# Two transformer layers on one core: weight loads on a second queue, and two buffers moved

## The chip, the cores and the metric

The kernel runs on one core of a Trainium2 chip. A core has five engines, each with its own in-order stream of instructions: TensorE (PE in the profile, matrix products), VectorE (DVE), ScalarE (ACT), GpSimd (POOL) and SyncE (SP), which here issues the transfers between memory and the core. The metric is the device time of one execution in microseconds (us); less is better.

## The reference

Two layers, each an attention block and a feed-forward block, on 2048 rows of 640 numbers:

```python
def _A_ref(x, wqkv, wo):
    H = 32; Dh = D // H; W = 256
    ...
    scores = jnp.einsum("bhqd,bhkd->bhqk", q, k) * (Dh ** -0.5)
    mask = (idx[:, None] - idx[None, :] >= 0) & (idx[:, None] - idx[None, :] < W)
    p = _softmax(jnp.where(mask[None, None], scores, -1e9), axis=-1)
    o = jnp.einsum("bhqk,bhkd->bhqd", p, v)
    return o.transpose(0, 2, 1, 3).reshape(B, S, D) @ wo

def _B_ref(x, w1, b1, w2, b2):
    h = jnp.einsum("bsd,df->bsf", x, w1) + b1
    r = jnp.where(h > 0, h, 0)
    return jnp.einsum("bsf,fd->bsd", r * r, w2) + b2

x = x + _A_ref(_layernorm(x), A_wqkv, A_wo)
x = x + _B_ref(_layernorm(x), B_w1, B_b1, B_w2, B_b2)
```

The last two lines are done twice with the same weights. There are 32 heads of 20 numbers, the window is 256 keys, and the feed-forward width is 1536.

## The kernel before

**Tiling.** The rows are worked on in 16 units of 256 (eight a layer). A unit goes through these stages: layernorm and transposition of its rows (`ln_load`, `ln_t`), query and key products (`stage_qk`), value products (`stage_v`), attention, output product (`stage_o`), second layernorm (`stage_y`) and feed-forward (`stage_f`). Every operand is kept as a pair of 16-bit numbers, high and low part, and every product is made as three (`mm3`, line 256), so each product's result is evicted twice: ScalarE writes the high part, VectorE the low part.

**Attention.** Heads go by fours ("quads", eight a unit). For a quad `max_quad` makes the scores, and VectorE takes the row maxima (line 555). After two quads `max_out` turns the maxima and sends them as two more rows of the queries (line 580). Then `exp_quad` makes the scores anew, less their maxima, ScalarE takes the exponential (line 625), GpSimd masks it (lines 640, 644), and `pv_quad` multiplies by the values (line 674). Scores of both kinds share one pair of memory banks, `bb`. Units 0 and 8 have no unit before them and half as many scores.

**Queries and keys** must change their layout, and do so by way of memory. `leave` (lines 435 to 468) writes the evicted tile `qd` out with two transfers (lines 445, 447) and reads it back with two others (line 451) into `qt` and `kt`. `qd` is a buffer of which there is one. In unit 0 the queries use it, while the keys use part of `hraw`; in units 1 and 2 queries and keys use it one after the other. For later units the keys have a place of their own.

**Output.** `load_o` reads a unit's attention output and its row sums (lines 720, 721), divides (753, 756) and splits into `od` (760, 763), which `stage_o` multiplies by the output weights. For unit 0 `od` lies in `hraw`, columns 1280 to 2560. So its load waits for the third and fourth piece of w2, which were staged there.

**Weights** come as 32-bit numbers into staging places and are converted into pairs (`convert`: ScalarE, then VectorE, or ScalarE again and GpSimd). The attention weights come first. The output weights (five pieces of 320 KB, line 224) and w1 (six of 640 KB, line 232) are staged in the room of w2, and w2 (twelve of 320 KB, line 245) in `hraw`: four places for the first four pieces, then two. `hraw` has the same memory as `hh`, the result of the first feed-forward product, so unit 0's `hh` waits for the last conversion. All of these loads are issued by SP, in between the transfers above.

**Order.** The order of the instructions on each engine is set by a planner in the kernel's own text, which runs when the program is built. `post` puts a job (engine, assumed duration, what it waits for, priority; a lower number goes first) on a list, and `pump` issues what is ready by its clocks. `dma` posts a transfer on SP, whose rate is an assumed number (`rate`); `idle` holds one back until SP's assumed transfers are nearly through. Waits for a buffer to come free are not in this plan: the engine meets them when it runs. TensorE's work is written by generators: `rest` is the chain of projections of units 0 to 2, and `flow` runs unit 0's quads and takes work from `rest` where a quad isn't ready. From unit 1 on `together` deals one unit's quads out evenly over the dense work of its neighbours, which for unit 1 is: what is left of `rest`, then `stage_o(0)`, `stage_y(0)` and `stage_f(0)`. From unit 4 on the rows are transposed by DMA (`ln_cross`, line 355), which `stage_f` starts between its two products; units 0 to 3 are transposed on TensorE (line 300).

The order of quads in unit 0, with m for `max_quad`, r for `max_out`, s for `exp_quad`, v for `pv_quad`, is:

```python
todo = [("m", n) for n in range(GQ)] + [("r", 0)] + [("m", n) for n in range(GQ, LEAD)]
for n in range(NQ):
    todo += [("s", n)] + ([("r", n + LEAD - GQ)] if n % GQ == 1 else []) + [("m", n + LEAD), ("v", n)]
flow(todo, rest)
load_o(0, False, (w2j[2], w2j[3]))
```

with GQ = 2, LEAD = 3 and NQ = 8: quads 8, 9 and 10, the first three of unit 1, have their maxima between unit 0's last quads.

Of the kernel before, what the change touches and what calls it, by code (L numbers as in the profile page):

```python
# [14 lines left out]
ALU = mybir.AluOpType  # L15
# [29 lines left out]
def kernel(ctx: ExitStack, tc: tile.TileContext, x, wqkv, wo, w1, b1, w2, b2, out):  # L45
# [45 lines left out]
    now, clk, pend, moved = [0.0], {"A": 0.0, "D": 2e3, "G": 0.0, "S": 0.0}, [], [0.0]  # L91
    LOOK, LAT, LAND, CROSS, WLAND = 250.0, 50.0, 1800.0, 3600.0, 4500.0
    rate = [335.0]
    TAIL = {"A": 115.0, "D": 85.0, "G": 40.0, "S": 0.0}

    class Job:
        def __init__(self, eng, cost, fn, deps, nb, prio, size=0, idle=False, land=LAND):
            self.eng, self.cost, self.fn, self.deps, self.nb, self.prio = eng, cost, fn, deps, nb, prio
            self.size, self.idle, self.land = size, idle, land
            self.end, self.gates = None, []  # L100
# [4 lines left out]
        def start(self):  # L105
            t = max([clk[self.eng], self.nb] + [d.end + LAT for d in self.deps])
            return max(t, moved[0] - 2200.0) if self.idle else t

        def put(self):
            t = self.start() + self.cost  # L110
            self.fn()
            clk[self.eng] = t
            self.end = t + TAIL[self.eng]
            if self.eng == "S":
                moved[0] = max(moved[0], t) + self.size / rate[0]
                self.end = moved[0] + self.land
            for g in self.gates:
                g.end = self.end
# [73 lines left out]
    def convert(st, hi, low, n, load, *deps, prio=2, dve=True):  # L192

        a = post("A", 20 + 0.9 * n, lambda: nc.scalar.activation(hi, st, AF.Copy, scale=WS), load, *deps, prio=prio)
        if dve:
            return post("D", 30 + 1.04 * n, lambda: nc.vector.scalar_tensor_tensor(low, st, WS, hi, op0=ALU.mult,
                                                                                   op1=ALU.subtract), a, prio=prio)
        b = post("A", 20 + 0.9 * n, lambda: nc.scalar.activation(st, st, AF.Copy, scale=WS), a, prio=prio)
        return post("G", 30 + 2.0 * n, lambda: nc.gpsimd.tensor_tensor(low, st, hi, op=ALU.subtract), b, prio=prio)
# [20 lines left out]
    def load_wo():  # L220
        v = wo.rearrange("(h c d) n -> c d h n", c=KC, d=4)
        for c in range(KC):
            st = w2raw[:, FC * D - (KC - c) * D:][:, :D]
            load = dma(lambda st=st, c=c: nc.sync.dma_start(st, v[c]), P * D * 4, gate0, prio=2, idle=True, land=WLAND)
            woj[c] = convert(st, wo_s[:, 0, c], wo_s[:, 1, c], D, load, dve=False)
        rowset[1] = [post("D", 460, lambda k=k: set_row(1, k), prio=2) for k in range(4)]

    def load_w1():
        first = list(wqj.values())
        for f0 in (0, 6, 2, 8, 4, 10):  # L230
            st = w2raw[:, f0 * D:(f0 + 2) * D].rearrange("p (c n) -> p c n", c=KC)
            load = dma(lambda st=st, f0=f0: nc.sync.dma_start(
                st, w1[:, f0 * P:(f0 + 2) * P].rearrange("(c p) n -> p c n", p=P)), P * KC * 2 * P * 4, gate,
                *(woj.values() if (f0 + 2) * D > (FC - KC) * D else ()), prio=2, idle=True, land=WLAND)
            for f in (f0, f0 + 1):
                c = slice(f * P, (f + 1) * P)
                w1j[f] = convert(st[:, :, (f - f0) * P:(f - f0 + 1) * P], w1_s[:, 0, :, c], w1_s[:, 1, :, c], KC * P,
                                 load, *first, dve=f % 3 == 2)

    def load_w2():  # L240
        for c in range(FC):
            first = [w1j[f] for f in (c // 4 * 2, c // 4 * 2 + 1, 6 + c // 4 * 2, 7 + c // 4 * 2)]
            slot = c if c < 4 else c % 2
            st = hraw[:, D * slot:D * (slot + 1)]
            load = dma(lambda st=st, c=c: nc.sync.dma_start(st, w2[c * P:(c + 1) * P, :]), P * D * 4,
                       *([w2j[c - 4 if c < 6 else c - 2]] if c > 3 else [gate]), prio=2, idle=True,
                       land=WLAND)
            w2j[c] = convert(st, w2_s[:, 0, c], w2_s[:, 1, c], D, load, *first, dve=c % 3 == 2)
# [136 lines left out]
    def stage_qk(u, which=(0, 1)):  # L385
# [7 lines left out]
        for j, c0 in order:  # L393
            if j not in qds:
                if j == 0:
                    qts[u] = sb.tile([P, NP, T], F16, name="qt", tag="qt", bufs=2)
                if j and u == 0:
                    qd = hraw[:, :KC * T].bitcast(F16).rearrange("p (c a n) -> p c a n", a=2, n=T)
                elif j and u > 2:
                    qd = beside(u)[:, 1].rearrange("p (c a n) -> p c a n", a=2, n=T)  # L400
                else:
                    qd = sb.tile([P, KC, 2, T], F16, name="qd", tag="qd", bufs=1)
                qds[j] = qd
# [299 lines left out]
    def load_o(u, late=False, free_=()):  # L703
# [45 lines left out]
        for i in range(4):  # L749
# [15 lines left out]
            j = post("D", 575, ratio, loaded, prio=2)  # L765
            j = post("D", 409, times, j, prio=2)
            j = post("A", 360, high, j, prio=0 if i < 2 else 2)
            js.append(post("D", 402, low, j, prio=2))
# [6 lines left out]
    def stage_o(u):  # L775
        od, x1b, js, xj = ols.pop(u)
        for i in range(2):
# [15 lines left out]
            x1s[u, i], ys[u, i] = x1, (y, layernorm(x1, y, *adds, prio=1))  # L793
# [177 lines left out]
    def flow(todo, dense):  # L971
# [3 lines left out]
        while todo:  # L975
# [4 lines left out]
                     "v": quad[1][0] if quad else []}[kind]  # L980
# [24 lines left out]
    rate[0] = 215.0  # L1005
    ln_load(1)
# [18 lines left out]
    left_over = 3 * (QKC + VC + LNC) - used[0]  # L1025
    rate[0] = 320.0
    for u in range(1, NU):
        last = u == NU - 1
        quads, ahead = range(NQ * u, NQ * (u + 1)), range(NQ * u + LEAD, NQ * (u + 1) + LEAD)
# [50 lines left out]
```

## Time and profile before

| | |
|---|---|
| median of three runs | 1644.63 us (1643.55 to 1646.98) |
| the profiled execution | 1641.93 us |
| its span, first to last instruction | 1640.2 us |
| mean granted clock of TensorE | 0.987 |
| busy: TensorE, VectorE, ScalarE, GpSimd | 96%, 63%, 46%, 39% |

The profile is that of one execution. Times within it count from the span's start. A line such as `L414` is that of the kernel's text; `qd<-acc` means that the tile qd was written from the tile acc; `x20` counts instructions; what stands in brackets behind an instruction is how long its engine was idle before it, and what ended that. SPq is SP's queue, where the time of a transfer is that of its issue, not of the bytes. In a table of stretches each engine has its busy time and its count, and the last three numbers are TensorE's granted clock (1.00 is full), the share of the transfer engines' time, and GB/s.

### The profile page before, as it was taken

Reading aid. Unit: us, or ns where it says so; the run is one execution under the profiler, and the core shown is the slowest. Engines: PE = TensorE matmul, PEld = TensorE weight load, DVE = VectorE, ACT = ScalarE, POOL = GpSimd, SP = SyncE. Lnnn points to the kernel's source line nnn. Section 1 sums busy time; section 2 is a strip of 40 time slices with the busy share of each in tenths; the row PEclk is TensorE's granted clock in tenths of the full one; section 3 lists DMA queues with packets and bytes.
Section 4 is the critical chain, followed back from the end, with each engine's and each line's share of the span. In section 5 each row is a group of like instructions: output and inputs, shape, how many; then the busy total and the mean of one; then the engine's idle time right before and its main releaser. Section 6 shows DMA issues by size and latency. Waiting matters only on the chain.

```text
span 1640.2 us, 52819 instructions
## 1 busy us (share of the span) xinstructions
PE 1575.6 (96%) x21670; PEld 1172.6 (71%) x21670; DVE 1030.1 (63%) x3231; ACT 748.4 (46%) x1616; POOL 636.6 (39%) x1309
## 2 busy tenths in 40 slices
PE   7697899999999999999999999999999999999989
PEld 5564677777777777777777777777777777776667
DVE  7567657675665766566565756657665666757341
ACT  4465534535444454544434354444545444453512
POOL 1343533535344353434414343443534344354412
PEclk9898999999999999999999999999999999999999
DMA  8465214343342434345253434425343452431020
GB/s 255 123 183 157 62 63 109 65 118 86 102 102 65 124 75 112 80 108 114 51 137 74 124 85 103 102 69 119 73 112 81 106 117 51 110 71 54 27 65 17
DMA packets 231517, 157.95 MB, mean 96 GB/s; under 512 B 79468, under 2 KB 215020, under 8 KB 231276
## 3 DMA queue, kind: packets, MB, share of 16 engines
q1 hardware_dynamic: 231276, 154.59, 38.4%
q8 instruction: 170, 2.79, 0.7%
q14 instruction: 71, 0.58, 0.1%
HBM read 84.68 MB, written 52.95 MB: 84 GB/s over the span
## 4 chain that ended last, share of the span: by engine, by line
PE 83%; DVE 6%; ACT 4%; DMA 4%; POOL 2%; issue 1%; SPq 1%; DVEq 0%; ACTq 0%; POOLq 0%
PE acc L256 63%; PE pv L674 10%; PE bb L542 5%; PE bb L613 5%; DVE bb L555 3%; ACT pt L625 2%; DMA qk<-qd 1%; DMA xt<-in_B_b_dram 1%; PE tr L567 1%; POOL x L805 1%; DVE mx L555 1%; POOL pt L644 0%; ACT r L843 0%; DMA w_s<-in_B_w_dram 0%; DMA ov<-o 0%
## 5 line engine op out<-in xcount | busy, mean ns | idle before, releaser
L555 DVE CUSTOM_DVE_ANT_0 bb<-bb,maskb 128x384 f32<-128x384 f32 (+2 forms) x1024 | 510.5, 567 | 114.9 <-PE bb L542 106.4
L625 ACT ACTIVATE pt<-bb 128x512 f32<-128x512 f32 (+1 forms) x736 | 376.5, 601 | 233.9 <-PE bb L613 220.5
L640 POOL TENSOR_SCALAR_AFFINE_SELECT pt<-pt 128x256 f32<-128x256 f32 x448 | 194.8, 439 | 529.7 <-ACT pt L625 507.9
L256 PE MATMUL acc<-y,w_s 128*128 128x256 f16 x2880 | 330.8, 273 | 4.8 <-DVE y L304 1.5
L256 PE MATMUL acc<-w_s,hh 128*128 128x320 f16 x2304 | 326.2, 299 | 0.0
L256 PEld LDWEIGHTS <-w_s 128*128 128x128 f16 x2880 | 277.9, 98 | 57.3 <-issue 23.5
L256 PE MATMUL acc<-yT,wq_s 128*128 128x256 f16 x2400 | 281.0, 275 | 14.0 <-DVE qd L414 11.9
L256 PEld LDWEIGHTS <-hh 128*128 128x128 f16 x2304 | 221.7, 98 | 96.8 <-issue 12.5
L256 PEld LDWEIGHTS <-wq_s 128*128 128x128 f16 x2400 | 232.9, 99 | 57.5 <-issue 26.5
L644 POOL TENSOR_SCALAR_AFFINE_SELECT pt<-pt 128x256 f32<-128x256 f32 x512 | 217.3, 446 | 65.7 <-ACT pt L625 64.6
L853 DVE TENSOR_TENSOR hh<-r,hh 128x256 f16<-128x256 f32 x192 | 91.9, 500 | 205.9 <-ACT hh L850 199.3
L674 PE MATMUL pv<-pt,vt 128*32 128x128 f32 (+1 forms) x3840 | 189.6, 332 | 2.0 <-POOL pt L644 1.4
L847 POOL TENSOR_TENSOR r<-r 128x256 f32<-128x256 f32 x192 | 113.5, 612 | 181.2 <-ACT r L843 179.9
L686 ACT COPY ot<-pv 128x256 f32<-128x256 f32 x128 | 47.6, 372 | 277.4 <-PE pv L674 277.4
L555 DVE DVE_READ_ACCUMULATOR2_ANT mx<- 128x1 f32 x1024 | 145.4, 142 | 0.1
L256 PE MATMUL acc<-wq_s,yT 128*128 128x320 f16 x960 | 142.1, 301 | 0.1
L674 PEld LDWEIGHTS pv<-pt,vt 128*32 128x32 f32 x3840 | 104.4, 110 | 45.6 <-POOL pt L644 4.9
L256 PE MATMUL acc<-wo_s,od 128*128 128x320 f16 x900 | 130.5, 299 | 3.9 <-DVE x L785 1.7
L843 ACT ACTIVATE r<-acc,b1s 128x256 f32<-128x256 f32 x192 | 80.6, 471 | 98.0 <-PE acc L256 97.2
L256 PEld LDWEIGHTS <-yT 128*128 128x128 f16 x960 | 93.1, 99 | 40.4 <-issue 6.5
L256 PEld LDWEIGHTS <-od 128*128 128x128 f16 x900 | 85.5, 98 | 44.7 <-issue 8.3
L613 PE MATMUL bb<-qt,kt 62*64 62x128 f16 (+3 forms) x3840 | 100.3, 235 | 9.1 <-DVE mx L555 8.4
(84 smaller groups left out, 1169.5 us busy)
## 6 DMA issues: line engine op xcount, KB each, us to landing
qt<-qk SPq DMA_DIRECT2D x30, 480.0 KB
kt<-qk SPq DMA_DIRECT2D x30, 480.0 KB
qk<-qd SPq DMA_DIRECT2D x17, 640.0 KB
o<-ot SPq DMA_DIRECT2D x256, 42.0 KB
od<-o SPq DMA_DIRECT2D x13, 640.0 KB
qk<-yl SPq DMA_DIRECT2D x13, 640.0 KB
qk<-qd SPq DMA_DIRECT2D x17, 320.0 KB
xt<-in_A_x_dram SPq DMA_DIRECT2D x16, 320.0 KB
```

What stands on the lines that cost most here:

```text
L256: nc.tensor.matmul(acc, lhs(a, c), rhs(b, c), start=(k == 0), stop=(k == 3 * nk - 1))
L542: nc.tensor.matmul(to, qt[r, p, i * P + 64 * h:i * P + 64 * h + 64], kt[r, p, a:b], start=True, stop=True, tile_position=(64 * e, 64 * h))
L555: nc.vector.tensor_tensor_reduce(out=v, in0=v, in1=mask, scale=1.0, scalar=-3.0e38, op0=ALU.add, op1=ALU.max, accum_out=accum)))
L613: nc.tensor.matmul(bb[e][64 * h:64 * h + 64, k, o:o + w], kt[r, p, ko + 64 * h:ko + 64 * h + 64], qt[r, p, q:q + w], start=True, stop=True ...
L625: nc.scalar.activation(box["pt"][:, :o], bb[e][:, k, :o], AF.Exp, scale=SCALE / (QS * QS))
L640: nc.gpsimd.affine_select(out=m, in_=m, pattern=[[0, 2], [-1, P]], compare_op=ALU.is_gt, fill=0.0, base=0, channel_multiplier=1)
L644: nc.gpsimd.affine_select(out=m, in_=m, pattern=[[0, 2], [1, P]], compare_op=ALU.is_ge, fill=0.0, base=0, channel_multiplier=-1)
L674: nc.tensor.matmul(pv[32 * jj:32 * (jj + 1), q0 * P:(q0 + qn) * P], vf[:, c:c + 32], pj[:, j, :], start=(k == 0), stop=(k == len(steps) - ...
L686: nc.scalar.copy(ot[:, qd % 2], pv)
L843: nc.scalar.activation(box["r"], acc[:, f, :], AF.Relu, bias=b1s[:, f0 + f:f0 + f + 1], scale=1.0 / (YS * WS))
L847: nc.gpsimd.tensor_tensor(box["r"], box["r"], box["r"], op=ALU.mult)
L853: nc.vector.tensor_sub(hh[:, 1, f, :], box["r"], hh[:, 0, f, :])
```

## The change

1. Unit 0's queries too are evicted into `hraw`, behind the keys' part.
2. Output weights, w1 and w2 are issued by ScalarE, through the new `wdma`. The planner keeps a second clock of moved bytes for that queue, with a rate of 100 bytes a ns, a landing time of 6000 ns instead of 4500 and 400 ns of slack ahead of the conversions. SP's transfers are taken to land 2000 ns later until unit 1 is done. The first output weight no longer goes at the earlier gate (unit 0's first keys), but at that of its last. w2 is staged in four places throughout.
3. Unit 0's `od` is a tile in `qd`'s buffer, and its load no longer waits for two conversions. The division and both layernorms around it have a better priority, and so has the layernorm of the rows of units 1 and 2.
4. The first three maxima of unit 1 and their `max_out` stand behind unit 0's last quad and behind `load_o(0)`, not between unit 0's quads.
5. Unit 2's second half of the value products leaves `rest` and goes into `stage_y(0)`, a quarter ahead of each of the two rows' transposes. Unit 3's rows are no longer transposed on TensorE; `stage_f(0)` starts their `ln_cross`.

```diff
-    rate = [335.0]
+    rate = {"S": 335.0, "A": 100.0}
+    late_ = [0.0]
...
-            return max(t, moved[0] - 2200.0) if self.idle else t
+            return max(t, moved[self.eng] - 2200.0) if self.idle else t
...
-            if self.eng == "S":
-                moved[0] = max(moved[0], t) + self.size / rate[0]
-                self.end = moved[0] + self.land
+            if self.size:
+                moved[self.eng] = max(moved[self.eng], t) + self.size / rate[self.eng]
+                self.end = moved[self.eng] + late_[0] if self.eng == "S" else t + self.size / 200.0
+                self.end += self.land
...
+    def wdma(fn, size, *deps):
+
+        return post("A", 450.0, fn, *deps, prio=2, size=size, idle=True, land=WLAND)
...
-            load = dma(lambda st=st, c=c: nc.sync.dma_start(st, v[c]), P * D * 4, gate0, prio=2, idle=True, land=WLAND)
+            load = wdma(lambda st=st, c=c: nc.scalar.dma_start(st, v[c]), P * D * 4, gate)
...
-            load = dma(lambda st=st, f0=f0: nc.sync.dma_start(
+            load = wdma(lambda st=st, f0=f0: nc.scalar.dma_start(
...
-            slot = c if c < 4 else c % 2
+            slot = c % 4
...
-            load = dma(lambda st=st, c=c: nc.sync.dma_start(st, w2[c * P:(c + 1) * P, :]), P * D * 4,
-                       *([w2j[c - 4 if c < 6 else c - 2]] if c > 3 else [gate]), prio=2, idle=True,
-                       land=WLAND)
+            load = wdma(lambda st=st, c=c: nc.scalar.dma_start(st, w2[c * P:(c + 1) * P, :]), P * D * 4,
+                        *([w2j[c - 4]] if c > 3 else [gate]))
...
-                if j and u == 0:
-                    qd = hraw[:, :KC * T].bitcast(F16).rearrange("p (c a n) -> p c a n", a=2, n=T)
+                if u == 0:
+                    qd = hraw[:, (1 - j) * KC * T:][:, :KC * T].bitcast(F16).rearrange("p (c a n) -> p c a n", a=2, n=T)
...
-            od = hraw[:, 2 * D:4 * D].bitcast(F16).rearrange("p (c a n) -> p c a n", a=2, n=T)
+            od = sb.tile([P, KC, 2, T], F16, name="od", tag="qd", bufs=1)
...
+            pr = 2 if u else 0.5
+            j = post("D", 575, ratio, loaded, prio=pr)
+            j = post("D", 409, times, j, prio=pr)
+            j = post("A", 360, high, j, prio=0 if i < 2 else pr)
+            js.append(post("D", 402, low, j, prio=pr))
...
-    def stage_y(u):
+    def stage_y(u, between=()):
...
+            if between:
+                yield from stage_v(*between[i])
...
     def ahead_of(u):
         yield from stage_qk(u)
-        yield from stage_v(u)
-        yield from ln_t(u + 1)
+        yield from stage_v(u, range(4 if u < 2 else 2))
         if u < 2:
-            ln_load(u + 2)
+            yield from ln_t(u + 1)
+        if u < 1:
+            ln_load(u + 2, prio=1.5)
...
-        todo += [("s", n)] + ([("r", n + LEAD - GQ)] if n % GQ == 1 else []) + [("m", n + LEAD), ("v", n)]
+        todo += [("s", n)] + [("r", n + LEAD - GQ)] * (n % GQ == 1 and n + LEAD - GQ < NQ)
+        todo += [("m", n + LEAD)] * (n + LEAD < NQ) + [("v", n)]
+    todo += [("o", 0)] + [("m", NQ + n) for n in range(GQ)] + [("r", NQ)] + [("m", NQ + n) for n in range(GQ, LEAD)]
     flow(todo, rest)
-    load_o(0, False, (w2j[2], w2j[3]))
...
-            parts += [rest, stage_o(0), stage_y(0)]
+            parts += [rest, stage_o(0), stage_y(0, ((2, (2,)), (2, (3,))))]
             cost += LNC + left_over
+            ahead_ln = 3
```

In `flow` the new kind "o" calls `load_o(0)`.

More of the change, by code (lines that the diff above doesn't have):

```diff
@@ L86, with __init__ @@
         set_row(0, k)
-    now, clk, pend, moved = [0.0], {"A": 0.0, "D": 2e3, "G": 0.0, "S": 0.0}, [], [0.0]
-    LOOK, LAT, LAND, CROSS, WLAND = 250.0, 50.0, 1800.0, 3600.0, 4500.0
-    rate = [335.0]
+    now, clk, pend, moved = [0.0], {"A": 0.0, "D": 2e3, "G": 0.0, "S": 0.0}, [], {"S": 0.0, "A": 0.0}
+    LOOK, LAT, LAND, CROSS, WLAND, SLACK = 250.0, 50.0, 1800.0, 3600.0, 6000.0, 400.0
+    rate = {"S": 335.0, "A": 100.0}
+    late_ = [0.0]
     TAIL = {"A": 115.0, "D": 85.0, "G": 40.0, "S": 0.0}
     class Job:
-        def __init__(self, eng, cost, fn, deps, nb, prio, size=0, idle=False, land=LAND):
+        def __init__(self, eng, cost, fn, deps, nb, prio, size=0, idle=False, land=LAND, slack=0.0):
             self.eng, self.cost, self.fn, self.deps, self.nb, self.prio = eng, cost, fn, deps, nb, prio
-            self.size, self.idle, self.land = size, idle, land
+            self.size, self.idle, self.land, self.slack = size, idle, land, slack
             self.end, self.gates = None, []
@@ L105, in start @@
         def start(self):
-            t = max([clk[self.eng], self.nb] + [d.end + LAT for d in self.deps])
-            return max(t, moved[0] - 2200.0) if self.idle else t
+            t = max([clk[self.eng], self.nb] + [d.end + LAT + self.slack for d in self.deps])
+            return max(t, moved[self.eng] - 2200.0) if self.idle else t
         def put(self):
@@ L192, in convert @@
     def convert(st, hi, low, n, load, *deps, prio=2, dve=True):
-        a = post("A", 20 + 0.9 * n, lambda: nc.scalar.activation(hi, st, AF.Copy, scale=WS), load, *deps, prio=prio)
+        slack = SLACK if prio > 1 else 0.0
+        a = post("A", 20 + 0.9 * n, lambda: nc.scalar.activation(hi, st, AF.Copy, scale=WS), load, *deps, prio=prio,
+                 slack=slack)
         if dve:
             return post("D", 30 + 1.04 * n, lambda: nc.vector.scalar_tensor_tensor(low, st, WS, hi, op0=ALU.mult,
-                                                                                   op1=ALU.subtract), a, prio=prio)
+                                                                                   op1=ALU.subtract), a, prio=prio,
+                        slack=slack)
         b = post("A", 20 + 0.9 * n, lambda: nc.scalar.activation(st, st, AF.Copy, scale=WS), a, prio=prio)
-        return post("G", 30 + 2.0 * n, lambda: nc.gpsimd.tensor_tensor(low, st, hi, op=ALU.subtract), b, prio=prio)
+        return post("G", 100 + 2.2 * n, lambda: nc.gpsimd.tensor_tensor(low, st, hi, op=ALU.subtract), b, prio=prio,
+                    slack=slack)
     wqj, woj, w1j, w2j = {}, {}, {}, {}
@@ L231, in load_w1 @@
             st = w2raw[:, f0 * D:(f0 + 2) * D].rearrange("p (c n) -> p c n", c=KC)
-            load = dma(lambda st=st, f0=f0: nc.sync.dma_start(
+            load = wdma(lambda st=st, f0=f0: nc.scalar.dma_start(
                 st, w1[:, f0 * P:(f0 + 2) * P].rearrange("(c p) n -> p c n", p=P)), P * KC * 2 * P * 4, gate,
-                *(woj.values() if (f0 + 2) * D > (FC - KC) * D else ()), prio=2, idle=True, land=WLAND)
+                *(woj.values() if (f0 + 2) * D > (FC - KC) * D else ()))
             for f in (f0, f0 + 1):
@@ L763, in low @@
                 nc.vector.tensor_sub(od[:, :, 1, q], val[:, :, q], od[:, :, 0, q])
[L765 to L768, printed above, removed]
+            pr = 2 if u else 0.5
[3 more added lines that the diff above has]
+            js.append(post("D", 402, low, j, prio=pr))
         ols[u] = od, x1, js, xj
@@ L792, in stage_o @@
             y = sb.tile([P, D], F32, name="xt", tag="xt", bufs=2)
-            x1s[u, i], ys[u, i] = x1, (y, layernorm(x1, y, *adds, prio=1))
+            x1s[u, i], ys[u, i] = x1, (y, layernorm(x1, y, *adds, prio=1 if u else 0.5))
     def add_b2(u):
@@ L979, in flow @@
                      "s": [*bbjobs, *([rowjobs.get((u, G))] if n % GQ == 0 else [])],
-                     "v": quad[1][0] if quad else []}[kind]
+                     "v": quad[1][0] if quad else [], "o": []}[kind]
             if not all(j is not None and j.end is not None and j.end <= now[0] + LOOK for j in wants):
@@ L990, in flow @@
                 max_quad(n)
+            elif kind == "o":
+                load_o(0)
             elif kind == "r":
@@ L1004 @@
     run(ln_t(0))
-    rate[0] = 215.0
-    ln_load(1)
+    rate["S"] = 215.0
+    late_[0] = 2000.0
+    ln_load(1, prio=1.5)
     load_wo()
@@ L1021 @@
     for n in range(NQ):
-        todo += [("s", n)] + ([("r", n + LEAD - GQ)] if n % GQ == 1 else []) + [("m", n + LEAD), ("v", n)]
+        todo += [("s", n)] + [("r", n + LEAD - GQ)] * (n % GQ == 1 and n + LEAD - GQ < NQ)
+        todo += [("m", n + LEAD)] * (n + LEAD < NQ) + [("v", n)]
+    todo += [("o", 0)] + [("m", NQ + n) for n in range(GQ)] + [("r", NQ)] + [("m", NQ + n) for n in range(GQ, LEAD)]
     flow(todo, rest)
-    load_o(0, False, (w2j[2], w2j[3]))
-    left_over = 3 * (QKC + VC + LNC) - used[0]
-    rate[0] = 320.0
+    left_over = 3 * (QKC + VC) + 2 * LNC - used[0]
+    rate["S"] = 320.0
     for u in range(1, NU):
         last = u == NU - 1
+        if u > 1:
+            late_[0] = 0.0
         quads, ahead = range(NQ * u, NQ * (u + 1)), range(NQ * u + LEAD, NQ * (u + 1) + LEAD)
```

## The prediction

> **What bounds the kernel now.** I read the page's engine shares and slices first, then the busy time by stages, then what TensorE waited for, then the chain and the queues around each wait.
>
> ```profile
> span 1640.2 us, 52819 instructions
> ...
> PE   7697899999999999999999999999999999999989
> ```
>
> TensorE is full from the sixth slice on; the open time lies in the first 200 us. By stages (busy time of the engines, then TensorE's granted clock, DMA share, GB/s):
>
> ```profile
> 36.00:58.00 22.00, 20.22 (x261) 15.06 (x260) 18.07 (x83) 8.91 (x19) 5.47 (x8) 1.00 0.52 131
> 58.00:70.00 12.00, 0.38 (x3) 0.26 (x3) 1.09 (x3) 2.30 (x6) 0.52 (x2) 0.56 0.39 140
> 70.00:101.00 31.00, 29.39 (x363) 20.15 (x362) 16.11 (x77) 20.21 (x45) 15.14 (x24) 0.95 0.73 172
> 101.00:127.00 26.00, 20.95 (x313) 15.63 (x314) 21.10 (x66) 15.84 (x30) 12.07 (x16) 0.93 0.51 164
> 127.00:145.00 18.00, 16.13 (x206) 10.36 (x195) 9.89 (x27) 13.04 (x27) 9.67 (x17) 0.90 0.55 162
> 145.00:176.00 31.00, 21.34 (x237) 12.74 (x237) 23.16 (x61) 12.21 (x24) 9.11 (x15) 0.73 0.64 154
> 176.00:198.00 22.00, 20.37 (x302) 16.61 (x302) 11.26 (x35) 15.77 (x36) 15.71 (x28) 1.00 0.09 25
> 260.00:1640.00 1380.00, 1359.49 (x18929) 1016.72 (x18927) 861.14 (x2685) 619.39 (x1353) 543.73 (x1142) 1.00 0.37 88
> ```
>
> Span less the first figure is TensorE's idle time: 11.6, 1.6, 5.0, 1.9, 9.7 and 1.6 us in the six stages from 58 to 198, 31.4 in all. The lowered clock costs at most busy time times what is missing of 1.00: 1.5 + 1.5 + 1.6 + 5.8 = 10.4 us between 70 and 176. So about 42 us lie there to be won; the last stage, 1380 us at 98.5% and full clock, is not touched by the diff. What TensorE waited for up to 260 us (total, times, longest):
>
> ```profile
> PE acc L256 <- DVE qd L414: 11.9, 1, 11.9
> ...
> PE bb L613 <- DVE mx L555: 4.9, 4, 3.0
> PE acc L256 <- ACT stg L760: 4.1, 1, 4.1
> PE tr L300 <- DVE xt L286: 3.1, 1, 3.1
> PE acc L256 <- DVE stg L763: 2.9, 2, 2.1
> ```
>
> **Term 1, the hole at 58 (weights leave SP's queue).** The timelines of SP and ScalarE, and the chain of waits:
>
> ```profile
> 49.38 1.79 SPq L224 DMA_DIRECT2D w_s<-in_A_wo_dram  x3
> 51.22 0.94 SPq L232 DMA_DIRECT2D w_s<-in_B_w_dram  x1
> 52.37 5.42 SPq L445 DMA_DIRECT2D qk<-qd  x1
> 57.83 3.27 SPq L447 DMA_DIRECT2D qk<-qd  x1
> ```
>
> ```profile
> 68.24 0.60 ACT L411 ACTIVATE qd<-acc 128x512 f16<-128x512 f32 x1 [9.70 <-DMA qk<-qd]
> ```
>
> ```profile
> 108.22 6.17 DMA qk<-qd
> ```
>
> Unit 1's queries and keys share the one buffer qd: the first key eviction waits until the query write has left it, ScalarE and VectorE stand behind it in order, and TensorE with both accumulators full. The write was issued behind 1.6 MB of weights and was out only at 68.1; unit 2's write, alone, took 6.2 us. The first edit (unit 0's queries in hraw) does not touch this pair: unit 1 still has one buffer. It only frees qd of unit 0's write, for which no wait shows. What helps is that the weights are elsewhere: issued at 52.4, the write is out near 59; with 0.60 for ScalarE and 0.7 for VectorE TensorE resumes near 60.4 instead of 69.6, having run dry at 57.7. I add 1 us for weights moving beside it: hole 3.7, **gain 8.0**. Ends: 0 (the same bytes finish as late) and 11.6.
>
> **Term 2, 101 to 145 (maxima of unit 1 behind load_o).**
>
> ```profile
> 126.20 0.27 PE L613 MATMUL bb<-qt,kt 62*64 62x256 f16 x1 [3.02 <-DVE mx L555]
> ```
>
> ```profile
> 121.53 0.86 PE L542 MATMUL bb<-kt,qt 60*64 60x128 f16 x36
> ```
>
> ```profile
> 101.00:145.00 44.00, 17.13 (x64) 0.92 0.53 163
> ```
>
> ```profile
> 29.83 6.82 PE L256 MATMUL acc<-wq_s,yT 128*128 128x320 f16 x49
> ```
>
> The second row is one quad's score products, the third VectorE's work at L555 alone: 64 instructions, four quads, 4.3 us a quad. Before, three of these quads lay between unit 0's quads with projection work beside them. Now they stand in a row: 12.9 us of VectorE against 3 x 0.86 = 2.6 us of score products and the half of unit 2's values left in the stream, 30 products of 0.139 us = 4.2. That exposes 6.2 us where 3.3 showed. The transposes of unit 3 leave, with their waits of about 1.1. Together a **loss of 1.8**. Ends: a loss of 7 (no filler stands there), a gain of 6.9 (all hidden). The wait of 1.6 for unit 2's query write stays.
>
> **Term 3, 145 to 176 (od's own place, values ahead of the transposes).**
>
> ```profile
> 124.70 1.58 SPq L691 DMA_DIRECT2D o<-ot  x4
> ...
> 135.53 2.20 SPq L245 DMA_DIRECT2D stg<-in_B_w_dram  x2
> 137.83 0.59 SPq L720 DMA_DIRECT2D rs<-o  x1
> ```
>
> Unit 0's last output left at 126.3, but its load came 11.5 us later, behind w2's loads and for two conversions whose staging od took. Both go. I keep 2 us for landing: 9.5 us earlier. TensorE also arrives earlier at the output product: 4.2 for the values moved away, 2.8 for the transposes and their waits; and later by the maxima now between, 2.6 + 2.9. Net 8.0 us, against 7.0 of waits for od; I leave 1 open. New in its way: od now lies in qd and waits for unit 2's key write; that was issued at 129.4, before load_o, so the load's trip covers it; uncovered it costs the 6.2 above. y2 follows od there, but only after y's layernorm. The values in front of each transpose give 15 products, 2.0 us, against the 3.1 us wait for y: 1.1 left. Idle 9.7 to 2.6, **gain 7.1**; ends 0 and 9.7.
>
> **Term 4, the smaller parts.** Unit 3's ten transposes leave TensorE:
>
> ```profile
> 141.37 0.49 PE L300 MATMUL tr<-ident,xt 128*128 128x128 f32 x3
> 142.42 0.44 PE L300 MATMUL tr<-ident,xt 128*128 128x128 f32 x2 [0.56 <-ACT vt L480]
> 143.39 0.83 PE L300 MATMUL tr<-ident,xt 128*128 128x128 f32 x5 [0.53 <-DVE yT L304]
> ```
>
> **1.7 us gained.** In exchange come two loads of x and four DMA transposes in stage_f(0), hidden behind its second product as for every later unit. w2 comes by four slots throughout: of the 1.6 us at 176 to 198 I count **0.5** (ends 1.6, and a loss of 3 if it comes late). The first output weight, held to the later gate, starts some 1 us later, far ahead of its use: nothing.
>
> The weights' issues go to ScalarE (ns: least, median, most):
>
> ```profile
> L224 SPq DMA_DIRECT2D w_s<-in_A_wo_dram x5: 537/579/707, 35.4 to 50.6; - x5
> L232 SPq DMA_DIRECT2D w_s<-in_B_w_dram x6: 394/399/942, 51.2 to 105.4; - x6
> L245 SPq DMA_DIRECT2D stg<-in_B_w_dram x12: 327/357/1843, 108.8 to 179.7; - x12
> ```
>
> 5 x 0.58 + 6 x 0.40 + 12 x 0.36 = 9.6 us. ScalarE is busy 72.5 of the 140 us from 36 to 176, and behind each issue, and each wait for a staging slot, stand exponentials and evictions. Most fall into its idle half: **cost 1**; ends 0 and 9.6.
>
> **Term 5, the clock.**
>
> ```profile
> 114.00:118.00 4.00, 2.37 (x30) 1.73 (x28) 2.88 (x6) 2.44 (x4) 1.82 (x2) 0.94 0.03 10
> 118.00:122.00 4.00, 3.94 (x47) 2.66 (x48) 2.69 (x7) 3.06 (x8) 2.62 (x5) 0.63 0.01 1
> ```
>
> In the hole from 58 to 70 the clock was 0.56, and 1.6 us of idle time (114 to 118) were enough for 0.63 in the 4 us behind. I let the loss go with idle time: from 58 to 176 there were 29.8 us, left are 3.7 + 1.6 + 8.7 + 2.6 = 16.6; 10.4 x 13.2 / 29.8 = **4.6 gained**; ends 0 and 10.4. The Trainium skill (TensorE: Matmul & The Clock Gate, "What's actually happening") has the clock fall only after a whole idle window of about 3.4 us; by that of what is left only term 1's hole would cost, and the gain would be some 4 us more. The row of 118 to 122, behind 1.6 us, speaks against it.
>
> **Sum.** 8.0 - 1.8 + 7.1 + 1.7 + 0.5 - 1 + 4.6 = 19.1. The profiled execution took 1641.93 us (1.7 around its span); the median of the three runs is 1644.63. Less 19.1 that is 1622.8 by the profiled execution and by the median **1625.5 us**, which I give.
>
> **Rivals.** *A, the transfers share the engines.* The write need not stand behind the weights to be slowed by them: 2.62 MB (1.64 of weights, 0.98 of queries) moved from 49.4 to 68.1, 0.140 MB a us. If the write of 0.98 MB gets half, it takes 14 us, is out at 66.4, and term 1 gives 1.7 and the clock 2.2 less: gain 10.6, 1634. For it: 0.39 of the DMA time was used and yet 140 GB/s moved. Against: 6.17 us in the other row. The Trainium skill (DMA: Bandwidth & Descriptors, "Issuing engines are not separate DMA queues") says that DMAs issued from several engines run on the same 16 and that this saves only the time of issue; by that term 1 would be this rival's. No run shows two queues yet.
>
> *B, slower: ScalarE stands in its own issues.* L445 above held SP 5.42 us with 1.6 MB queued ahead. ScalarE has 67.5 us free from 36 to 176; 23 issues of 2.9 us use it up, and from there the kernel is slower. At 3.5 us each it is 13 us: 1658. Against: the loads are spaced at 100 bytes a ns, and the median issue is 0.4.
>
> *C, everything is covered.* Only 3 us of term 1 and the 1.6 of unit 2 remain: 42 + 1.7 - 4.6 - 1.6 for their clock - 1 = 36: 1608. For it: TensorE has other work at each wait. Against: VectorE's 4.3 us a quad.
>
> *D, the wait moves.* Term 2 loses 7 and term 3 gains only 2: 8 - 7 + 2 + 1.7 + 0.5 - 1 + 1 = 5: 1639.5.
>
> *E, A and D together*: nothing left.
>
> **Chances.** Forecast 0.50, A 0.13, C 0.13, D 0.09, E 0.06, B 0.09. The measurement tells 0.2% (3.3 us) from no change: faster 0.85, same 0.06, slower 0.09. The range from 1607 to 1643 takes in A, C and D and leaves out B and the ends of C and E.
>
> **What would show it.** Term 1: L445 short on SP, the wait of L411 for qk<-qd from 9.7 to 2-4 us (A: 8). Term 2: waits of L613 or L567 for mx over 3 us ahead of the first 32-product L613. Term 3: L720 within 6 us of the last o<-ot, and no wait for L760 or L763 over 2 us. ScalarE's queue: issues of 0.3 to 1 us (B: over 2.9). Term 5: 0.90 or more in all stages behind 70. A hole at a new place, or ScalarE late with exponentials, would prove the forecast wrong.

## The result and the profile after

| | median, us | lowest to highest |
|---|---|---|
| before | 1644.63 | 1640.89 to 1647.51 (5 runs) |
| after | 1654.66 | 1653.2 to 1656.54 (5 runs) |

The ratio is 1.0061, 95% interval 1.0042 to 1.0079: the changed kernel is slower by 10 us, where the forecast was 19 faster. The profiled execution has a span of 1652.4 us against 1640.2.

The stages of the prediction, in the same columns (idle time of TensorE is the first figure less the second), and the stretch from 225 to 260, which in the trace of before had 33.32 us of work:

```profile
36.00:58.00 22.00, 20.44 (x221) 16.39 (x219) 13.45 (x62) 4.43 (x10) 0.55 (x1) 1.00 0.68 167
58.00:70.00 12.00, 7.01 (x84) 4.57 (x82) 5.12 (x19) 5.81 (x11) 4.18 (x7) 0.81 0.57 127
70.00:101.00 31.00, 28.87 (x327) 19.71 (x325) 14.24 (x65) 19.81 (x40) 13.37 (x19) 0.91 0.62 164
101.00:127.00 26.00, 20.64 (x282) 13.93 (x275) 9.79 (x38) 18.86 (x39) 12.99 (x22) 1.00 0.60 186
127.00:145.00 18.00, 5.75 (x108) 3.98 (x107) 15.33 (x50) 5.24 (x11) 3.23 (x3) 0.50 0.67 168
145.00:176.00 31.00, 27.44 (x347) 18.72 (x349) 21.59 (x60) 18.83 (x38) 16.48 (x31) 0.91 0.50 136
176.00:198.00 22.00, 19.32 (x317) 15.39 (x310) 13.52 (x43) 14.82 (x33) 15.69 (x26) 1.00 0.13 40
225.00:260.00 35.00, 23.49 (x320) 16.71 (x318) 18.53 (x54) 10.97 (x22) 6.02 (x16) 0.80 0.32 76
```

Idle time went from 11.6 to 5.0 us at 58 and from 9.7 to 3.6 behind 145. But there are two new holes: 12.3 us at 127 (1.9 before), with a clock of 0.50, and 11.5 us at 225 (1.7 before), with 0.80. TensorE's waits up to 260 us (total, times, longest) name them:

```profile
PE bb L622 <- DVE mx L564: 10.7, 5, 3.8
PE acc L265 <- DMA yT<-yl: 10.6, 1, 10.6
```

**The hole at 58 shrank.** On SP the write of unit 1's queries is issued within 1 us (it held SP for 8.7 us before), ScalarE waits for it until 63.0, and TensorE loses 3.8 us to it (timelines of SP, ScalarE and TensorE):

```profile
54.35 0.38 SPq L454 DMA_DIRECT2D qk<-qd  x1
54.78 0.52 SPq L456 DMA_DIRECT2D qk<-qd  x1
```

```profile
63.00 0.60 ACT L420 ACTIVATE qd<-acc 128x512 f16<-128x512 f32 x1 [9.13 <-DMA qk<-qd]
```

```profile
64.37 1.37 PE L265 MATMUL acc<-yT,wq_s 128*128 128x256 f16 x10 [3.81 <-DVE qd L423]
```

**The hole at 127** is the row of maxima of unit 1's three quads. The last projection product that can stand between them is used up at 119, before the row begins. From there TensorE only follows VectorE, and the division of `od` stands behind the third quad on VectorE (timelines of TensorE and VectorE):

```profile
118.84 0.58 PE L265 MATMUL acc<-wq_s,yT 128*128 128x320 f16 x3
...
126.80 0.26 PE L551 MATMUL bb<-kt,qt 60*64 60x128 f16 x1 [3.92 <-DVE mx L564]
...
133.21 0.37 PE L576 MATMUL tr<-ident,mx 128*16 128x128 f32 x1 [4.41 <-DVE mx L564]
...
138.82 0.37 PE L622 MATMUL bb<-qt,kt 62*64 62x256 f16 x1 [3.81 <-DVE mx L564]
142.96 1.49 PE L622 MATMUL bb<-qt,kt 62*64 62x256 f16 x31 [3.77 <-DVE mx L564]
144.38 2.05 PE L265 MATMUL acc<-wo_s,od 128*128 128x320 f16 x7
```

```profile
138.63 0.96 DVE L762 RECIPROCAL rs<-rs 128x64 f32<-128x64 f32 x2
```

**The hole at 237** is unit 3's crossing (`ln_cross`: load, layernorm, split into two parts, four transposes by DMA). Its rows are asked for at 192.9, VectorE comes to the low part of the second 128 rows only at 235.9, and the last transpose stands on SP behind the load of x, which held SP 3.8 us (SP, VectorE and TensorE):

```profile
192.87 0.83 SPq L335 DMA_DIRECT2D xt<-in_A_x_dram  x2
...
230.36 3.98 SPq L364 DMA_TRANSPOSE yT<-yl  x3
...
236.42 3.80 SPq L744 DMA_DIRECT2D x<-in_A_x_dram  x2
...
241.56 1.39 SPq L364 DMA_TRANSPOSE yT<-yl  x1
```

```profile
235.93 0.82 DVE L361 TENSOR_TENSOR yl<-xt,yl 128x640 f16<-128x640 f32 x1
```

```profile
247.72 8.13 PE L265 MATMUL acc<-yT,wq_s 128*128 128x256 f16 x49 [10.63 <-DMA yT<-yl]
```

Unit 3's queries began at 235.2 before; now one product of them comes at 236.8 and the others from 247.7. These 12.5 us are about the difference of the spans (12.2), so what follows took equally long in both.

### The profile page after: what moved, and what is told of

Read it like the earlier page. It is cut to its first block, busy times and chain, and to the rows that moved or that the text cites. A ratio compares the mean times of both kernels' runs of the same rounds, so it can differ in the third digit from the quotient of the medians.

```text
span 1652.4 us, 52796 instructions
## 1 busy us (share of the span) xinstructions
PE 1577.2 (95%) x21660; PEld 1173.9 (71%) x21660; DVE 1026.4 (62%) x3229; ACT 749.7 (45%) x1614; POOL 635.0 (38%) x1309
## 4 chain that ended last, share of the span: by engine, by line
PE 83%; DVE 2%; ACT 2%; DMA 1%; POOL 0%; issue 0%; SPq 0%; DVEq 0%; ACTq 0%; POOLq 0%
PE acc L265 63%; PE pv L683 10%; PE bb L622 5%; PE bb L551 5%; ACT pt L634 1%; DVE bb L564 1%; PE tr L576 1%; ACT r L855 0%; DMA kt<-xs 0%; DMA yT<-yl 0%; DVE mT L581 0%; DVE mT L582 0%; DMA xs<-x 0%; POOL pt L653 0%; DVE hh L865 0%
## 5 line engine op out<-in xcount | busy, mean ns | idle before, releaser
L265 PE MATMUL acc<-yT,wq_s 128*128 128x256 f16 x2400 | 283.3, 277 | 16.6 <-DMA yT<-yl 10.6
L265 PEld LDWEIGHTS <-hh 128*128 128x128 f16 x2304 | 221.7, 98 | 96.7 <-issue 12.5
L265 PE MATMUL acc<-wo_s,od 128*128 128x320 f16 x960 | 141.1, 302 | 1.8 <-DVE x L795 1.7
L564 DVE DVE_READ_ACCUMULATOR2_ANT mx<- 128x1 f32 x1024 | 141.5, 138 | 0.0
L265 PEld LDWEIGHTS <-od 128*128 128x128 f16 x960 | 92.1, 99 | 46.5 <-issue 8.8
```

The source lines that it names most:

```text
L265: nc.tensor.matmul(acc, lhs(a, c), rhs(b, c), start=(k == 0), stop=(k == 3 * nk - 1))
L564: nc.vector.tensor_tensor_reduce(out=v, in0=v, in1=mask, scale=1.0, scalar=-3.0e38, op0=ALU.add, op1=ALU.max, accum_out=accum)))
```

## The experiments

The column "against before" is the ratio to the runs of the kernel before on the same chip, less one, times 1644.6 us; a step between two rows is uncertain by some 3 us. The parts are those of the list in "The change"; "margin" is the 2000 ns by which part 2 makes the planner take SP's transfers to land later, until unit 1 is done.

| run | what it is | median, us | ratio, 95% interval | against before, us |
|---|---|---|---|---|
| after | all parts | 1654.66 | 1.0061 (1.0042 to 1.0079) | +10.0 |
| e1 | without part 5 | 1650.95 | 1.0040 (1.0026 to 1.0055) | +6.6 |
| e2 | all, unit 3's layernorm and crossing first | 1650.77 | 1.0039 (1.0024 to 1.0054) | +6.4 |
| e3 | without part 4 | 1648.84 | 1.0025 (1.0013 to 1.0036) | +4.1 |
| e4 | parts 1 to 3 | 1645.02 | 1.0009 (0.9999 to 1.0019) | +1.5 |
| e6 | all, no margin | 1643.44 | 0.9995 (0.9985 to 1.0004) | -0.8 |
| e7 | parts 1 to 3, no margin | 1647.58 | 1.0021 (1.0012 to 1.0031) | +3.5 |
| e8 | before, weights on ScalarE's queue | 1653.54 | 1.0047 (1.0032 to 1.0062) | +7.7 |
| e9 | before, short maxima in unit 0 | 1643.81 | 0.9994 (0.9984 to 1.0004) | -1.0 |
| e10 | e7 and two quads ahead | 1641.03 | 0.9979 (0.9968 to 0.9989) | -3.5 |
| e12 | e7, `od` in `hraw`, w2 in two places | 1653.41 | 1.0056 (1.0040 to 1.0072) | +9.2 |
| e13 | e12 and two quads ahead | 1652.25 | 1.0045 (1.0030 to 1.0061) | +7.4 |
| e14 | e6, `od` in free room | 1635.68 | 0.9945 (0.9928 to 0.9963) | -9.0 |
| e15 | e14 without part 4 | 1631.22 | 0.9921 (0.9906 to 0.9936) | -13.0 |
| e17 | e7, `od` in free room | 1638.85 | 0.9965 (0.9954 to 0.9977) | -5.8 |
| e18 | e10, `od` in free room | 1638.82 | 0.9962 (0.9948 to 0.9977) | -6.2 |
| e19 | all, `od` in free room | 1654.87 | 1.0057 (1.0041 to 1.0073) | +9.4 |
| e21 | e15 and two quads ahead | 1631.62 | 0.9923 (0.9896 to 0.9950) | -12.7 |

### Parts 4 and 5, one by one

e1 (part 5 undone: unit 3 transposed on TensorE, all of unit 2's values in `rest`):

```diff
-        yield from stage_v(u, range(4 if u < 2 else 2))
+        yield from stage_v(u)
+        yield from ln_t(u + 1)
         if u < 2:
-            yield from ln_t(u + 1)
-        if u < 1:
-            ln_load(u + 2, prio=1.5)
+            ln_load(u + 2, prio=1.5 if u < 1 else 2)
...
-            parts += [rest, stage_o(0), stage_y(0, ((2, (2,)), (2, (3,))))]
+            parts += [rest, stage_o(0), stage_y(0)]
-            ahead_ln = 3
```

> The fifth part of the change alone undone: unit 3's rows on TensorE again, all of unit 2's values back in the stream. Theory: the changed kernel's wait of 10.6 us for yT<-yl at 237 us comes from unit 3's crossing being finished late, and with its lowered clock (2.5 us) it goes; 1.7 us of transposes come back: 1654.7 - 11 = about 1643. Rival (ScalarE's queue makes the transfers late everywhere): another wait of similar size takes its place, within 3 us of 1654.7.

e2 (the changed kernel, with the jobs of unit 3's layernorm and crossing at priority 0.5 instead of 2):

> The changed kernel, with a better priority (0.5, not 2) for unit 3's layernorm and crossing alone. Theory (the crossing is late because VectorE's and ScalarE's steps for it stand behind maxima and exponentials): the wait for yT<-yl falls from 10.6 to under 4 us, 1654.7 - 9 = about 1646. Rival (it is late because the last transfer stands behind the x loads on SP, or because ScalarE's weights slow the transfers): the wait stays over 8 us, time within 3 us of 1654.7.

e3 (part 4 undone, `load_o` left where it is):

```diff
-        todo += [("m", n + LEAD)] * (n + LEAD < NQ) + [("v", n)]
-    todo += [("o", 0)] + [("m", NQ + n) for n in range(GQ)] + [("r", NQ)] + [("m", NQ + n) for n in range(GQ, LEAD)]
+        todo += [("m", n + LEAD), ("v", n)]
+    todo += [("o", 0)]
```

> The fourth part alone undone: unit 1's first maxima between unit 0's quads again, load_o(0) still at the end of unit 0. Theory: the idle time from 123 to 143 us (16 us in five waits for VectorE's maxima) falls to under 6 and the clock there comes back, about 14 us: 1641. Rival (VectorE bounds that stage whatever the order): the same idle time appears between unit 0's quads, within 4 us of 1654.7.

e4 (both undone):

> Parts four and five both undone, so the first three parts remain (queries by the staging buffer, weights on ScalarE's queue, own place for the divided output, with the better priorities). Theory: both holes go, 1654.7 - 25 = about 1630, under the kernel before by 15. Rival (the first three parts give nothing): 1642 to 1648, as before.

Each hole could be taken away by itself, and each time other waits grew or a new one came. In e1 and in e2 no wait for `yT<-yl` is left, but TensorE's waits for the maxima are longer than the 10.7 of the changed kernel (e1, then e2):

```profile
PE bb L622 <- DVE mx L564: 14.9, 5, 9.3
```

```profile
PE bb L623 <- DVE mx L565: 17.2, 9, 5.4
```

In e3 the row of maxima is gone and `od` is what is late, with the hole for yT still there:

```profile
PE acc L265 <- DMA yT<-yl: 11.0, 1, 11.0
PE acc L265 <- ACT od L769: 10.7, 1, 10.7
```

So e1, e2 and e3 gained 3.4, 3.6 and 5.9 us where 9 to 14 were expected. e4, parts 1 to 3 alone, is as fast as the kernel before, as its rival had it: with the hole at 58 smaller and parts 4 and 5 undone nothing was gained, and TensorE waits 7.3 us for `od`. The first theory, that parts 4 and 5 eat a gain which parts 1 to 3 bring, falls.

### Where the gain of the first hole goes

e7 (e4 without the margin):

```diff
-    late_[0] = 2000.0
```

> Parts one to three alone, as in the run before with both others undone (1645.0), and without the planner's 2000 ns of later landing on SP. Theory of the chain (the stretch to the output product is as long as unit 0's first scores, its eight quads and the round trip of its output, whatever TensorE waits for in between): the margin is what lets the first maxima start at 42.5 us instead of 36.6; without it they start near 37, the output product some 5 us earlier, time about 1640. Rival (waits add up one by one): a margin of the plan costs nothing by itself, within 2 us of 1645.

e8 (before, with part 2 but for the margin and w2's four places: `wdma`, its clock, the slack, the later gate, and a longer assumed time for GpSimd's conversions that the list of parts does not name):

> The kernel before with its later weights on ScalarE's queue and nothing else of the change (no margin). The prediction's way of adding: the hole at 58 us falls from 11.6 to about 4, gain 8 and some clock: about 1635. Theory of the chain: the hole falls as much, but TensorE waits as much longer for unit 0's divided output, within 3 us of 1644.6, less what the quads themselves come earlier.

e9 (before, where unit 0's maxima are taken over 64 columns only):

```diff
+                if u == 0:
+                    v, mask = (bb[e][:, 2, 3 * P:3 * P + 64] if w == 3 else bb[e][:, w, 3 * P - 64:3 * P]), maskb[:, P:P + 64]
```

> The kernel before, with unit 0's row maxima taken over 64 columns only, not 128 and 256 (the rest of the maximum is left out). That takes about 0.07 and 0.2 us off four instructions each, 1.1 us a quad, 8.6 us over the eight. Theory of the chain: unit 0's quads come through 6 to 9 us earlier and the time falls by 4 to 8 us, to 1637 to 1641, though TensorE is not named as waiting for these. Rival (waits add up; the hole at 58 and the late load of the output are what counts): less than 2 us.

e10 (e7, with unit 1's first two quads written behind `load_o(0)`, ahead of the output product):

```diff
     todo += [("o", 0)]
+    for n in range(NQ, NQ + 2):
+        todo += [("s", n)] + [("r", n + LEAD - GQ)] * (n % GQ == 1) + [("m", n + LEAD), ("v", n)]
```

> As the kernel without the margin, and two of unit 1's quads are put ahead of the output product, into the time in which its operand is on the way, not behind it. Theory of the chain: two quads are some 5 us of products that fill a wait which is there anyway, so 4 us under the kernel without the margin, about 1636. Rival (VectorE is what bounds there): no gain over it, within 2 us, since the quads' maxima delay the division.

e9 changed nothing: 8.6 us less of VectorE's time for the maxima, with the planner's assumed times as they were, do not speed unit 0 up. In e7 and e8 unit 0's last value product came at 113.0 and 113.5, 9 us ahead of the 122.3 of before, and both kernels were slower all the same. e8 was slower than either of its forecasts. In it the load of `od` still waits for two conversions and was issued at 143.8 (137.8 before), and w2 is late; TensorE's waits:

```profile
PE acc L264 <- ACT stg L768: 11.4, 1, 11.4
PE pv L682 <- ACT r L851: 7.3, 1, 7.3
```

In e7 the load went at 119.7. But `od` lies in `qd`'s buffer, out of which unit 2's keys were written only at 131.6. ScalarE's first write to `od` waits for that, VectorE waits in order behind it, and TensorE behind the maxima that stand there (SP, ScalarE, VectorE, TensorE's waits):

```profile
119.69 0.60 SPq L729 DMA_DIRECT2D rs<-o  x1
...
131.63 0.82 SPq L456 DMA_DIRECT2D qk<-qd  x1
```

```profile
138.45 0.46 ACT L769 CAST od<-kt 128x320 f16<-128x320 f32 x1 [7.73 <-DMA qk<-qd]
```

```profile
138.94 0.90 DVE L772 TENSOR_TENSOR od<-kt,od 128x320 f16<-128x320 f32 x2 [7.76 <-ACT od L769]
```

```profile
PE bb L622 <- DVE mx L564: 12.8, 1, 12.8
```

e10 puts two quads into this hole and gains 7 us on e7. The second theory is therefore a wait for a free buffer that part 3 made.

### The buffer and the margin

e12 (e7, `od` back in `hraw`, w2 staged in the two other places) and e13 (e12 with e10's two quads):

```diff
-            od = sb.tile([P, KC, 2, T], F16, name="od", tag="qd", bufs=1)
+            od = hraw[:, 2 * D:4 * D].bitcast(F16).rearrange("p (c a n) -> p c a n", a=2, n=T)
...
-            slot = c % 4
+            slot = c % 2
```

> The kernel of e7_no_margin with unit 0's od back in hraw, columns 1280 to 2560, so that it no longer waits for unit 2's key write in qd; w2 is staged in the other two places throughout. Theory (the 12.8 us hole of e7 is the wait for a free buffer that the move to qd made): VectorE's L772 no longer stands 7.8 us for od L769, no wait of L622 for mx L564 over 4 us between 125 and 150, TensorE idles under 8 us there instead of 13, and the time falls from 1647.6 to 1636-1641. Rival (od's rows are late anyway, or two staging places make w2 late): the hole turns into a wait for od or into one of L682 for r at 180-200, and the time stays at 1644-1649.

> The kernel of e12 with two of unit 1's quads ahead of the output product, as in e10_two_more (1641.0). Theory: the two mend the same hole from two sides, so together they give little more than the better one: 1635-1640. Rival (each mends its own wait): the gains add, 6.5 from the quads on top of e12. If w2 in two places is late, 1641-1646.

These two could not tell: with two places w2 came late, and the hole moved behind 176, in e12:

```profile
PE pv L683 <- ACT r L855: 15.1, 1, 15.1
```

e6 (the changed kernel with only the margin taken out):

> The changed kernel with the 2000 ns landing margin for SP's transfers taken out and nothing else. Theory (the margin holds unit 0's first maxima 6 us back, so the hole at 58 is given back before it is used): v of quad 7 comes at 113-115 instead of 120-121, both holes that parts 4 and 5 open stay, at 115-140 and 230-245: 1646-1651 against 1654.7. Rival (the margin costs nothing, or the earlier arrival meets unit 2's key write in qd as in e7): 1652-1658.

e14 (e6 with `od` where w2's last two pieces will lie; they are converted after the output product):

```diff
-            od = sb.tile([P, KC, 2, T], F16, name="od", tag="qd", bufs=1)
+            od = w2_s[:, :, FC - 2:].rearrange("p a c n -> p a (c n)").rearrange("p a (c n) -> p c a n", n=T)
...
-        for f0 in (0, 6, 2, 8, 4, 10):
+        for f0 in (0, 6, 4, 10, 2, 8):
```

> The kernel of e6_margin_alone with unit 0's od in the room of w2's pieces 10 and 11 instead of qd's buffer; these two are converted only after the output product, four staging places for w2 stay, and w1's third and fourth load are those of the room that od takes. Theory (VectorE stands in order behind od, which waits 11.3 us on ScalarE and 7.6 on VectorE for unit 2's key write): od's first L769 comes at 119-123 instead of 131.2, the wait of 17.6 for mx falls to 5-10, and the time from 1643.4 to 1633-1638. Rival (three quads' maxima in a row, 12.9 us of VectorE, keep the hole whatever od does): the wait stays over 13, and the time at 1641-1645.

e15 (e14 without part 4), e17 (e7 with e14's place) and e18 (e10 with e14's place):

> e14 with part 4 undone too (the maxima of unit 1 between unit 0's quads). Theory (part 4's cost is the row of maxima with no filler, whatever the margin): 3-6 us faster than e14. Rival (early maxima use up VectorE's time and the filler that the output product's wait needs): within 2 us of e14 or slower.

> The kernel of e7_no_margin (parts 1 to 3 without the margin) with unit 0's od in the room of w2's pieces 10 and 11. Theory (the 12.8 us hole of e7 is the wait of od for unit 2's key write in qd, which had issued only at 131.2): od's L769 at 127-130 instead of 138.5, no wait for mx over 4 us between 125 and 150, no late w2, and the time falls from 1647.6 to 1636-1641. Rival (something else late stands there): 1644-1649.

> The kernel of e10_two_more (1641.0; od's L769 at 129.7 after 1.7 us of waiting) with unit 0's od in the room of w2's pieces 10 and 11. Theory (little was left to wait for in qd): 1638-1641. If it falls below 1636, od's place costs more than the waits that name it.

e19 (e14 with the margin back) and e21 (e15 with e10's two quads):

> e14 with the landing margin of 2000 ns put back: the changed kernel with od in free room as the one difference. It makes the square of margin and od's place whole: after 1654.7, e6 (no margin) 1643.4, e14 (no margin, free room) 1635.7. Theory (with the margin unit 2's key write and od's load both come after the row of maxima, so od never waits for qd): 1652-1656, no gain from the place while the margin stands. Rival (the place costs its 8 us by itself): 1644-1649.

> e15 (1631.2) with two of unit 1's quads ahead of the output product, as in e10 and e18. Theory (its wait of 5.3 for mx near 138 has no filler, and the quads are one): 1627-1631. Rival (as from e17 to e18, where they gave nothing): 1630-1634.

**The margin** costs most of all that was taken out of the changed kernel singly: one line less gives back 10.8 us (e6 against the changed kernel). With it the planner writes its steps later. Unit 0's first score products for the maxima come at 42.4 with it and at 38.7 without, its last value product at 121 and at 105. But these 16 us are not where the time is won: from 101 to 145 TensorE idles 19.3 us in e6, where it was 17.6, and it reaches unit 3's queries at 236.2, where it was 236.8. What goes is the hole at 237; e6 waits for yT only twice 0.5 us there. The same stretch in e6:

```profile
225.00:260.00 35.00, 31.84 (x479) 22.96 (x479) 22.94 (x67) 15.14 (x32) 11.17 (x24) 1.00 0.50 120
```

Idle time there is 3.2 us instead of 11.5, and the clock is 1.00 instead of 0.80. Unit 3's rows are asked for later than in the changed kernel (208.4, not 192.9), and yet the last transpose is issued by 235.5, not 243. Which of its steps the margin holds up, no run tells. (e2 has no such wait either, but in it TensorE comes to unit 3's queries only at 245.1.) What the margin is worth depends on the rest: 18.4 us with `od` in free room (e19 against e14), and nothing in parts 1 to 3 alone, where e7 is 2 us slower than e4.

**The place of `od`** costs nothing while the margin stands: e19 is the changed kernel again. Without the margin it costs 8.2 us (e14 against e6) and 9.2 us (e17 against e7). e6 shows why. The load of `od` is issued at 110.7, ahead of unit 2's keys, which leave `qd` at 120.3 and 121.6; ScalarE waits for them (SP, ScalarE, VectorE, TensorE's waits):

```profile
110.74 0.91 SPq L729 DMA_DIRECT2D rs<-o  x1
...
121.60 1.62 SPq L456 DMA_DIRECT2D qk<-qd  x1
```

```profile
131.19 0.46 ACT L769 CAST od<-kt 128x320 f16<-128x320 f32 x1 [11.31 <-DMA qt<-mT]
```

```profile
131.68 0.49 DVE L772 TENSOR_TENSOR od<-kt,od 128x320 f16<-128x320 f32 x1 [7.55 <-ACT od L769]
```

```profile
PE bb L622 <- DVE mx L564: 21.9, 3, 17.6
```

The trace of e6 names another transfer, qt<-mT, as what ended ScalarE's wait, that of e7 the write itself. That it is `qd` in e6 too is shown by e14, where nothing but the place of `od` and the order of w1 and w2 that makes room for it differ (in e19 the same edit cost and gained nothing). There the first write to `od` (the trace calls it w_s, whose room it has) comes at 123.3, and TensorE's wait at the same place is 10.9:

```profile
123.25 0.46 ACT L771 CAST w_s<-kt 128x320 f16<-128x320 f32 x1 [4.07 <-DVE kt L767]
```

```profile
133.06 2.01 PE L624 MATMUL bb<-qt,kt 62*64 62x256 f16 x32 [10.89 <-DVE mx L566]
```

**Part 4** costs 4.0 us there (e15 against e14, on one chip, 1631.1 to 1632.74 against 1634.62 to 1636.69). **Part 5** is a gain of 7.2 us once the margin and the buffer are out of its way (e15 against e17), though it made one of the two new holes in the changed kernel. The two quads of e10 give nothing on top of the free place (e18 against e17, e21 against e15), and the place only 2.7 us on top of them (e18 against e10): they filled the same hole.

e15 beats both kernels: 13 us faster than before, 23 faster than the changed one. In total its longest waits up to 260 us, besides one of 7.0 at the very start that the kernel before has too, are:

```profile
PE bb L624 <- DMA o<-ot: 6.4, 3, 5.1
PE bb L624 <- DVE mx L566: 5.5, 2, 5.3
PE bb L624 <- DMA qt<-mT: 3.9, 3, 2.1
```

## Why the prediction was wrong

**Term 1 had the size of its hole.** The wait was put at 3.7 us and was 3.8; with smaller waits beside it the stage idles 5.0, so 6.6 us were gained of 8.0. In part this is luck: TensorE ran dry at 60.6, not 57.7, and resumed at 64.4, not 60.4. The write was out 8.7 us after its issue, where rival A asked 14, but not because it passed the weights (see the last section). And the gain was counted as if the whole kernel became shorter by it, which e4 shows to be wrong.

**The margin had no term.** The planner's 2000 ns issue no instruction and add no wait, so the working, which priced instructions and waits, passed them over and so put them at nothing without a reason. They were the largest cost, 10.8 us, and term 4 is where they struck.

**Term 2 was wrong beyond its stated end.** It took 4.2 us of unit 2's values as filler and at worst a loss of 7. From 101 to 145 idle time rose from 6.9 to 17.6 us, by 10.7: no filler was left, and `od`'s division stood behind the maxima on VectorE. Of this part 4 is worth 4.0 us where it could be measured alone (e15 against e14).

**Term 3 was right in size at its place** (idle time 9.7 to 3.6; 2.6 was forecast), with no wait for `od` left. But the first output product came 4 us earlier, not 8, and TensorE had lost 12.3 us just ahead of it, in which `od` could get ready: the size is partly luck. The sentence that the trip of `od`'s load covers its wait for `qd` holds in the changed kernel, where the keys' write was issued at 114.8 and the load at 126.7. It does not hold in e6 and e7; the 6.2 us put on it uncovered are 8.2 and 9.2 there.

**Term 4's "hidden as for every later unit" was wrong**: TensorE waited 10.6 us for unit 3's rows. Later units were evidence only of the time that a later unit has; without the margin two waits of 0.5 are left (e6). TensorE also waited 2.7 us behind w2, near the stated end of 3. The issues on ScalarE took 0.33 to 0.54 us in the median, as reckoned:

```profile
L234 ACTq DMA_DIRECT2D w_s<-in_A_wo_dram x5: 537/540/1155, 47.4 to 71.7; - x5
L242 ACTq DMA_DIRECT2D w_s<-in_B_w_dram x6: 374/374/407, 77.1 to 119.5; - x6
L255 ACTq DMA_DIRECT2D stg<-in_B_w_dram x12: 334/335/532, 123.2 to 172.3; - x12
```

So rival B gave the right side by the wrong mechanism. Rival D had the right kind of thing, a wait that moves, but not the places: term 3 kept its gain, the hole at 237 is not in it, and it came out 5 us faster.

**Term 5** had the wrong sign, since idle time grew. By the same reckoning (busy time times what is missing of 1.00) the loss between 58 and 260 is 14.0 us against 10.5, so 3.5 more, not 4.6 less. Nor does idle time alone set the clock: this wait of 2.7 us, longer than the 1.6 on which the term rests, stands in a stage with a clock of 1.00.

```profile
189.44 1.51 PE L683 MATMUL pv<-pt,vt 128*32 128x256 f32 x32 [2.68 <-ACT r L855]
```

**From the forecast to the result** it is 29.1 us (19.1 faster forecast, 10.0 slower measured). Taken out one after the other, the margin is 10.8 of them (e6), the place of `od` 8.2 (e14) and part 4 4.0 (e15). With only the margin taken out the kernel is no faster than before, so the margin is the first step that failed and not the only one. The 6.1 us that e15 still lacks stay open.

The sum itself was the wrong form. Most terms are waits on one chain in a fixed order, and the experiments show how badly they add up: parts 1 to 3 give nothing, and the place of `od` gives nothing or 8 us according to a line elsewhere. The other assumed numbers of part 2 (the rate of 100 bytes a ns, the landing time of 6000 ns, the slack) stand in every run that has ScalarE's queue, so what they cost is not shown; e8, which has them without the margin, is 7.7 us slower than before.

## What to carry to other kernels

An assumed time in a planner is an edit like any other: ask what is written later because of it, and try the change without it. When a wait is removed in a chain of fixed order, do not add its length to the next gain; follow the chain to the next thing that has its own time (a conversion, a buffer that another step still holds, a row that is loaded late), and price the difference. A buffer shared "because the other user is done by then" is a bet on an order that every speed-up ahead of it can lose.

## What was not expected of the hardware

Loads issued by ScalarE got a queue of their own. The page lists the queues with packets, megabytes and share of the engines; before there was only q1, with 154.59 MB, and after:

```profile
q1 hardware_dynamic: 227640, 145.74, 37.0%
q10 hardware_dynamic: 6324, 9.50, 1.9%
```

The 9.50 MB are the weights. On SP the write of unit 1's queries held the engine no longer: 0.38 and 0.52 us for its two transfers, where it was 5.42 and 3.27. From the first issue to ScalarE's start it took 8.7 us (54.35 to 63.00), where the same 0.98 MB took 15.9 (52.37 to 68.24). But nothing shows that it passed the weights. The stretches from the first weight just ahead of the write to ScalarE's start, after and before:

```profile
47.40:63.00 15.60, 12.83 (x142) 10.70 (x141) 8.47 (x38) 1.58 (x4) 0.55 (x1) 1.00 0.38 128
```

```profile
49.30:68.20 18.90, 8.35 (x119) 6.18 (x118) 7.62 (x30) 4.98 (x10) 4.82 (x8) 0.77 0.48 139
```

After, 2.00 MB moved (15.60 us at 128 GB/s), and three weights and the write, issued in that time, are 1.97 MB. Before, 2.63 MB moved, and three output weights, a piece of w1 and the write are 2.62 MB. So in both kernels the write was out when all that had been issued by then, on either queue, had moved. The Trainium skill (DMA: Bandwidth & Descriptors, "Issuing engines are not separate DMA queues") says that transfers issued by several engines run on the same 16 DMA engines and that a second issuing engine saves only the time of issue; this trace agrees as far as it goes, though the profile lists a second queue. The shorter wait goes with fewer bytes of weights ahead (0.98 MB, not 1.64), as the planner now paces them. No run has the queue without the pace, so what the queue alone gives stays open.
